# Second expert products and output in two column halves, with four more early load tiles

## The chip, the cores and the metric

The kernel runs on one core of one Trainium2 chip. The metric is device time in microseconds (us) of one execution; before the change the median of three runs is 603.16 us (601.11 to 605.01). One further execution was profiled, and every row below is from it. Time zero of the rows is the start of its span.

## What is computed

Three parts follow each other: a chunked attention over 4 x 8 heads of 768 positions, a dense layer with a rational function in its middle (512 to 2048 to 512), and a soft mixture of 8 experts. The last part matters here:

```python
slot_input = d.T @ x                      # 32 slots, 4 of each expert
for e in range(8):
    h = np.maximum(slot_input[e] @ w1[e], 0.0)   # 512 -> 1024
    slot_out[e] = h @ w2[e]                      # 1024 -> 512
c = softmax over the 32 slots of x @ phi
return c @ slot_out                              # 3072 x 512
```

All is float32. The experts' weights are 16 MB of `w1` and 16 MB of `w2`, the output is 6.3 MB.

## The kernel before, in words

Tokens are worked in 6 blocks (NBLK) of 512. For each block PE forms the hidden layer in 8 steps, ACT, DVE and POOL evaluate the rational function, and a running softmax over tokens collects the slot sums in `u_acc`. The dense layer's output weights are narrowed to float32 early in block 0, step by step, and each step's 512 KB is parked in DRAM (`wo_dr`) by a DMA on POOL's queue; they are wanted again at the end.

From the first step of the last block on, everything that the end needs is loaded: 8 tiles of `wo_dr`, 32 of `w1`, 32 of `w2`, each 128 x 1024 floats (512 KB). They stand in one list (`wants`, the order in which PE uses them), and `fill` (L513 on) takes the next of the list for each buffer that the main loop gives back. The buffers are those of the ordinary pools (q, a4, k, v, xt, win, T, S, g), so a load waits until the last user of its buffer is done, in the order of the fills; SP issues all of them, with at most eight of its DMAs under way.

After the last block comes the end stage, and all of the change but the early loads lies here:

- L639 to L654: `u_acc` is turned, multiplied with the `wo` tiles and spread to the experts.
- L666: first products of the experts, `h1 = slot_input @ w1`, four experts beside each other in four groups of 32 columns of the PE array, in two rounds (`eq`) of four experts. L676/L678 take the positive part, L683 turns it, L685/L687 copy it out as `hts`.
- L693 and L701: second products with `w2`, 512 columns wide, four experts side by side; the last four `w2` tiles (L701) are worked in pieces of 256 columns as each of them lands.
- L705/L706 copy the result out in two column halves (W = 256), L709 adds the four groups through the constant matrix `stack`, L710/L711 copy that to `so4`.
- L724: for each block and pair of 128-token rows the output is `c_all` (32 slots) times `so4`; L729 (ACT) and L731 (DVE) scale it by `csum` on the way from PSUM to SBUF; L732 sends 128 x 1024 floats, 12 DMAs of 512 KB, in runs of 4 KB.

In the end stage before the change the tile scheduler orders the engines. PSUM is 8 banks of 512 floats a partition: pool `ps_h` two tiles of two banks, `ps_l` one bank, `ps_m` three.

In SBUF, 16 KB of each partition are set aside by default for descriptors of the DMAs that POOL issues (`wo_dr`).

Of the kernel before, what the change touches and what calls it, by code (L numbers as in the profile page):

```python
# [12 lines left out]
AF = mybir.ActivationFunctionType  # L13
ALU = mybir.AluOpType
# [30 lines left out]
def tile_chunk_attention__rational__soft_moe(  # L45
# [28 lines left out]
    NBLK = NT // BLK  # L74
    TT = BLK // P
# [15 lines left out]
    p_win = Pool(ctx.enter_context(tc.tile_pool(name="p_win", bufs=2 * NSTEP)))  # L91
    p_xt = Pool(ctx.enter_context(tc.tile_pool(name="p_xt", bufs=4)))
# [7 lines left out]
    p_s2 = Pool(ctx.enter_context(tc.tile_pool(name="p_s2", bufs=1)))  # L100
    p_dr = Pool(ctx.enter_context(tc.tile_pool(name="p_dr", bufs=1, space=bass.MemoryType.DRAM)))
    p_sm = Pool(ctx.enter_context(tc.tile_pool(name="p_sm", bufs=1)))
    ps_h = Pool(ctx.enter_context(tc.tile_pool(name="ps_h", bufs=2, space=PSUM)))
    ps_l = Pool(ctx.enter_context(tc.tile_pool(name="ps_l", bufs=1, space=PSUM)))
    ps_m = Pool(ctx.enter_context(tc.tile_pool(name="ps_m", bufs=3, space=PSUM)))

    def bank(shape):
        return ps_m("m", shape)
# [33 lines left out]
    xt = {}  # L142
# [165 lines left out]
    win = {}  # L308
# [66 lines left out]
    def soft1(b):  # L375
        lgs = p_s2("s2", [P, BLK])
        ACT.activation(lgs, st["lg"], AF.Copy)
        lt = bank([P, BLK])
        PE.matmul(lt, lhsT=stack, rhs=lgs, start=True, stop=True)
        ct = bank([P, TT, NSLOT])  # L380
        for tt in range(TT):
            PE.matmul(ct[:, tt, :], lhsT=lgs[:, tt * P:tt * P + P], rhs=stack[:, 0:NSLOT], start=True, stop=True)
        old, neg_m = (run[:, n:n + 1] for n in ((2, 0) if b % 2 else (0, 2)))
        bm, db = p_sm("bm", [P, 1]), p_sm("db", [P, 1])
        DVE.tensor_reduce(bm, lt, AX.X, ALU.max)
        if b == 0:
            DVE.tensor_scalar(neg_m, bm, -1.0, None, ALU.mult)
        else:
            DVE.tensor_scalar(neg_m, bm, -1.0, old, ALU.mult, ALU.min)
            ACT.activation(alpha, old, AF.Exp, bias=neg_m, scale=-1.0)  # L390
        pl = p_s2("s2", [P, BLK])
        ACT.activation(pl, lt, AF.Exp, bias=neg_m, accum_out=db)
        if b == 0:
            DVE.tensor_copy(den, db)
        else:
            DVE.scalar_tensor_tensor(den, den, alpha, db, ALU.mult, ALU.add)
        cm = p_sm("cm", [P, TT])
        ce = p_sm("ce", [P, TT, NSLOT])
        DVE.tensor_reduce(cm, ct, AX.X, ALU.max)
        DVE.tensor_tensor(ce, ct, cm.unsqueeze(2).to_broadcast([P, TT, NSLOT]), ALU.subtract)  # L400
        ACT.activation(ce, ce, AF.Exp)
        DVE.tensor_reduce(csum[:, b * TT:b * TT + TT], ce, AX.X, ALU.add)
        st["pl"], st["ce"] = pl, ce

    def soft2(b):
        pl = st.pop("pl")
        pb = bank([P, TT, NSLOT])
        for tt in range(TT):
            PE.transpose(pb[:, tt, :], pl[0:NSLOT, tt * P:tt * P + P], ident[0:NSLOT, 0:NSLOT])
        st["ptok"] = p_sm("ptok", [P, TT, NSLOT])  # L410
        ACT.activation(st["ptok"], pb, AF.Copy)  # L411

    def soft3(b):
# [196 lines left out]
    for kk in range(total + 4):  # L610
        b, i = divmod(kk, NSTEP)
        if kk == last:
            fill(p_q, "q", 1, 1)
            fill(p_a4, "a4", 2, 1)
            fill(p_k, "k", 1, 2)
            fill(p_v, "v", 1, 2)
            fill(p_xt, "xt", 2, 2)
        if i == 0 and b < NBLK - 1:
            state["att"] = attention_block(b + 1)
        for what in KN["ord0" if b == 0 else "ord" if b < NBLK - 1 else "ordz" if kk == total - 1 else "ordl"]:  # L620
            run_step(kk, what)
# [38 lines left out]
    for eq in range(2):  # L660
# [29 lines left out]
    for eq in range(2):  # L690
        for n in range(8 - 2 * eq):
            for j in range(4):
                PE.matmul(so[32 * j:32 * j + 32, :], lhsT=hts[eq][:, n, 32 * j:32 * j + 32],  # L693
                          rhs=got[("2", 4 * eq + j, n // 2)][:, n % 2, :],
                          start=(eq == 0 and n == 0), stop=False)
    W = DM // 2
    for j in range(4):
        for n in range(2):
            for w in range(2):
                g = (j + 2 * n + w) % 4  # L700
                PE.matmul(so[32 * g:32 * g + 32, W * w:W * w + W], lhsT=hts[1][:, 6 + n, 32 * j:32 * j + 32],  # L701
                          rhs=got[("2", 4 + j, 3)][:, n, W * w:W * w + W],
                          start=False, stop=(j == 3))
    sos, so4 = u_acc.rearrange("p (w d) -> p w d", w=2), p_s2("s2", [P, 2, W])
    ACT.activation(sos[:, 0], so[:, 0:W], AF.Copy)  # L705
    DVE.tensor_copy(sos[:, 1], so[:, W:])  # L706
    pb = [bank([P, W]) for _ in range(2)]
    for w in range(2):
        PE.matmul(pb[w], lhsT=stack, rhs=sos[:, w], start=True, stop=True)  # L709
    ACT.activation(so4[:, 0], pb[0], AF.Copy)  # L710
    DVE.tensor_copy(so4[:, 1], pb[1])  # L711
    rows = out.rearrange("(b r t) d -> b r t d", r=P, t=TT)
    for b in range(NBLK):
        for half in range(2):
            ob = p_win("win", [P, 2, DM])
            if half:
                pb = [bank([P, DM]) for _ in range(2)]
            else:
                both = ps_h("h", [P, 2, DM])
                pb = [both[:, m, :] for m in range(2)]  # L720
            for m in range(2):
                g = 32 * (2 * half + m)
                for w in range(2):
                    PE.matmul(pb[m][:, W * w:W * w + W], lhsT=c_all[g:g + 32, b, :], rhs=so4[g:g + 32, w, :],  # L724
                              start=True, stop=True)
            for m in range(2):
                n = TT * b + 2 * half + m
                if (m if b == 0 else half):
                    ACT.activation(ob[:, m, :], pb[m], AF.Copy, scale=csum[:, n:n + 1])  # L729
                else:  # L730
                    DVE.tensor_scalar(ob[:, m, :], pb[m], csum[:, n:n + 1], None, ALU.mult)  # L731
            SP.dma_start(out=rows[b, :, 2 * half:2 * half + 2, :], in_=ob)  # L732


_INS = ['qw', 'kw', 'vw', 'moe_w_in', 'moe_w_out', 'moe_a', 'moe_b', 'moe2_phi', 'moe2_w1', 'moe2_w2']
# [58 lines left out]
```

## Time and profile before

| | us |
|---|---|
| median of three runs | 603.16 |
| the profiled execution's own time | 600.04 |
| its span, from first to last instruction | 598.1 |
| PE busy | 546.8 (91% of the span) |
| DVE busy | 455.6 (76%) |
| ACT busy | 417.3 (70%) |

The profiled execution is 3.12 us under the median; 1.94 us of it lie outside the span. Rows of the timeline give a start, a duration, engine, line, operation, tiles and how many instructions were merged; in brackets the idle time before and what ended it. One float32 product of the source is two PE instructions, so 4 products are x8. Rows of windows give the stretch, its length, the busy time of each engine with its instructions, the clock granted to PE (1.00 is 2.4 GHz, 0.50 is 1.2 GHz), the share of the 16 DMA engines that is busy, and GB/s.

### The profile page before, as it was taken

The numbers are of one execution on the slowest core, as the hardware profiler recorded it, in microseconds if no ns is written. First come the engines' busy times: TensorE is split into PE (matmuls) and PEld (weight loads), VectorE is DVE, ScalarE is ACT, GpSimd is POOL, SyncE is SP. The second block draws the span as 40 slices with busy tenths as digits, with TensorE's granted clock in tenths as the row PEclk, the third lists the DMA queues.
The fourth block names the chain that finished last, engine by engine and source line by source line (L and its number), as shares of the span: only waits on it lengthen the run. The fifth ranks groups of instructions, "written<-read, shape, count | busy, mean of one in ns | idle before, by whom it ended". The sixth has DMA issues, their size and how long they took to land.

```text
span 598.1 us, 13663 instructions
## 1 busy us (share of the span) xinstructions
PE 546.8 (91%) x5944; PEld 390.4 (65%) x5944; DVE 455.6 (76%) x561; ACT 417.3 (70%) x542; POOL 124.6 (21%) x65
## 2 busy tenths in 40 slices
PE   6799699889999999999999999999999998779982
PEld 5677576667767777677776777766777576326241
DVE  4778999976987989978899798896987968711032
ACT  1589989976876868768687777777787869420032
POOL 0001221211322223122231313222133225200000
PEclk9699799888999999999999999999999999889996
DMA  8888674410221112212122022220374334799949
GB/s 351 354 327 322 256 291 185 147 66 1 107 73 66 61 53 106 73 42 80 58 107 73 15 93 72 107 71 3 106 276 156 132 118 158 290 358 411 408 184 360
DMA packets 21371, 97.41 MB, mean 163 GB/s; under 512 B 2624, under 2 KB 2752, under 8 KB 16320
## 3 DMA queue, kind: packets, MB, share of 16 engines
q1 hardware_dynamic: 20160, 92.35, 41.4%
q0 software_dynamic: 1152, 4.19, 1.7%
q8 instruction: 46, 0.75, 0.5%
q14 instruction: 13, 0.11, 0.1%
HBM read 86.05 MB, written 10.49 MB: 161 GB/s over the span
## 4 chain that ended last, share of the span: by engine, by line
PE 59%; DVE 14%; ACT 11%; DMA 8%; issue 4%; POOL 2%; SPq 0%; ACTq 0%; DVEq 0%; POOLq 0%
PE h L342 30%; PE m L368 4%; PE m L419 4%; PE lg L361 3%; ACT S L566 3%; ACT S L567 3%; PE m L224 3%; PE m L445 2%; DMA g<-in_moe_w_in_dram 2%; DVE T L580 2%; DVE T L579 2%; DMA g<-in_moe_w_out_dram 2%; PE h L666 2%; ACT g L369 2%; DVE S L568 2%
## 5 line engine op out<-in xcount | busy, mean ns | idle before, releaser
L342 PE MATMUL h<-xt,win 128*128 128x512 f32 x1152 | 293.4, 403 | 7.5 <-ACT win L325 5.3
L342 PEld LDWEIGHTS h<-xt,win 128*128 128x128 f32 x1152 | 212.1, 191 | 54.8 <-ACT win L325 6.7
L543 POOL TENSOR_TENSOR S<-S,S 128x1024 f32<-128x1024 f32 (+1 forms) x49 | 118.3, 2416 | 306.9 <-DVE S L568 288.8
L566 ACT ACTIVATE S<-h,ctab 128x1024 f32<-128x1024 f32 (+1 forms) x49 | 53.9, 1100 | 58.3 <-PE h L342 56.3
L568 DVE SCALAR_TENSOR_TENSOR S<-S,S 128x1024 f32<-128x1024 f32 (+1 forms) x49 | 58.8, 1200 | 41.0 <-ACT S L567 40.9
L579 DVE TENSOR_TENSOR T<-T,h 128x1024 f32<-128x1024 f32 (+1 forms) x49 | 58.4, 1191 | 6.6 <-ACT T L569 6.6
L596 DVE SCALAR_TENSOR_TENSOR T<-T,ctab,S 128x1024 f32<-128x1024 f32 (+1 forms) x49 | 63.3, 1294 | 0.0
L368 PEld LDWEIGHTS m<-ident,T 128*128 128x128 f32 x384 | 44.3, 144 | 27.9 <-issue 13.6
L597 DVE SCALAR_TENSOR_TENSOR T<-S,T 128x1024 f32<-128x1024 f32 (+1 forms) x49 | 59.8, 1219 | 3.2 <-POOL S L543 0.5
L580 DVE SCALAR_TENSOR_TENSOR T<-T,ctab,h 128x1024 f32<-128x1024 f32 (+1 forms) x49 | 61.2, 1250 | 0.7
L569 ACT ACTIVATE T<-h,ctab 128x1024 f32<-128x1024 f32 (+1 forms) x49 | 59.1, 1206 | 0.0
L586 ACT ACTIVATE S<-S,ctab 128x1024 f32<-128x1024 f32 (+1 forms) x49 | 55.9, 1140 | 0.8
L585 ACT ACTIVATE S<-S 128x1024 f32<-128x1024 f32 (+1 forms) x49 | 51.6, 1053 | 6.7 <-DVE S L568 4.9
L368 PE MATMUL m<-ident,T 128*128 128x128 f32 x384 | 54.1, 282 | 2.1 <-DVE a L185 1.4
L369 ACT ACTIVATE g<-m 128x512 f32<-128x512 f32 x96 | 53.4, 601 | 3.1 <-PE m L368 3.0
L567 ACT ACTIVATE S<-h,ctab 128x1024 f32<-128x1024 f32 (+1 forms) x49 | 54.1, 1104 | 0.6 <-DVE T L596 0.6
L361 PE MATMUL lg<-T,wp 128*32 128x512 f32 x192 | 38.9, 614 | 5.4 <-DVE T L597 5.3
L186 ACT ACTIVATE a<-a 128x512 f32<-128x512 f32 x22 | 13.8, 634 | 19.5 <-DVE a L185 19.5
L419 PE MATMUL m<-g,ptok 128*32 128x512 f32 x192 | 23.5, 634 | 0.4 <-ACT ptok L411 0.4
L333 POOL DMA_DIRECT2D wo<-win x8 | 4.7, 588 | 86.7 <-DVE win L303 67.3
L248 DVE TENSOR_TENSOR xt<-m,xt 128x512 fp32r<-128x512 f32 x24 | 16.3, 687 | 8.1 <-ACT xt L247 8.0
L247 ACT ACTIVATE xt<-m 128x512 fp32r<-128x512 f32 x24 | 14.3, 607 | 9.7 <-PE m L243 9.7
(163 smaller groups left out, 626.6 us busy)
## 6 DMA issues: line engine op xcount, KB each, us to landing
win<-in_moe_w_dram SPq DMA_DIRECT2D x32, 512.0 KB, 6.0
k<-in_kw_dram SPq DMA_DIRECT2D x11, 1024.0 KB, 7.2
v<-in_vw_dram SPq DMA_DIRECT2D x11, 1024.0 KB, 4.9
g<-in_moe_w_in_dram SPq DMA_DIRECT2D x8, 1024.0 KB, 5.7
g<-in_moe_w_out_dram SPq DMA_DIRECT2D x8, 1024.0 KB, 8.4
out_dram<-win SPq DMA_DIRECT2D x12, 512.0 KB, 5.0
q<-in_qw_dram SPq DMA_DIRECT2D x11, 512.0 KB, 4.1
T<-in_moe_w_dram SPq DMA_DIRECT2D x10, 512.0 KB, 9.7
```

Source lines behind the costliest of these rows:

```text
L342: PE.matmul(tile_[:, f2, :], lhsT=ww[:, c, f2 * P:f2 * P + P], rhs=xx[:, c, :], start=(n == 0), stop=(n == 3 * NC - 1))
L368: PE.transpose(pb[:, m, f2 * P:f2 * P + P], t_[:, f2, tt * P:tt * P + P], ident)
L369: ACT.activation(gts[b, qd][:, 2 * part:2 * part + 2, 2 * P * o:2 * P * o + 2 * P], pb, AF.Copy)
L543: POOL.tensor_tensor(out[:, o], q[:, o], w[:, o], ALU.mult)
L566: ACT.activation(s[:, o], hh[:, o], AF.Abs, scale=b0)
L567: ACT.activation(y[:, o], hh[:, o], AF.Square, scale=rb1)
L568: DVE.scalar_tensor_tensor(s[:, o], y[:, o], QC, s[:, o], ALU.add, ALU.add)
L569: ACT.activation(t[:, o], hh[:, o], AF.Identity, bias=a2, scale=a3)
L579: DVE.tensor_tensor(t[:, o], t[:, o], hh[:, o], ALU.mult)
L580: behind[kk] = DVE.scalar_tensor_tensor(t[:, o], t[:, o], a1, hh[:, o], ALU.add, ALU.mult).ins
L596: DVE.scalar_tensor_tensor(t[:, o], t[:, o], a0, w[:, o], ALU.add, ALU.mult)
L597: DVE.scalar_tensor_tensor(t[:, o], e[:, o], 2.0, t[:, o], ALU.subtract, ALU.mult, reverse0=True)
```

## The change

The end stage works the second products, their sum and the output in two column halves, `w` = 0 and 1, each 256 wide. All 16 groups of products of half 0 come first (`items(0)`), then four groups of half 1, the sum of half 0, and then six times two groups of half 1 and one output pass of half 0. After that comes half 1: copy, sum and six output passes. An output pass (`output(w, pair, u)`) is two blocks by two 128-row groups in one `ps_h` tile of two banks; ACT scales the part in one bank, DVE that in the other, and two DMAs of 256 KB are sent, in runs of 1 KB. The order of PE, ACT and DVE in this part is written out by hand (`manual_schedule`).

A pool `p_x` of four tiles is added. It is first in the list of fills, and its buffers have no earlier user. Its room comes from 15 KB less descriptor scratch (1024 bytes) and from two small tiles: `ce` now lives in its place in `c_all`, `ptok` in the tile of `pl`.

```diff
@@
+    p_x = Pool(ctx.enter_context(tc.tile_pool(name="p_x", bufs=4)))
@@ soft1, soft2
-        ce = p_sm("ce", [P, TT, NSLOT])
+        ce = c_all[:, b, :].rearrange("p (t s) -> p t s", t=TT)
-        st["ptok"] = p_sm("ptok", [P, TT, NSLOT])
+        st["ptok"] = pl[:, 0:TT * NSLOT].rearrange("p (t s) -> p t s", t=TT)
@@
         if kk == last:
+            fill(p_x, "x", 4, 1)
             fill(p_q, "q", 1, 1)
@@
-    so = ps_l("lg", [P, DM])
...
+    so = [ps_l("lg", [P, W]), bank([P, W])]
+    so4 = p_s2("s2", [P, 2, W])
+    def items(w):
+        cols = slice(W * w, W * w + W)
+        for eq in range(2):
+            for n in range(8 - 2 * eq):
+                for j in range(4):
+                    PE.matmul(so[w][32 * j:32 * j + 32, :], lhsT=hts[eq][:, n, 32 * j:32 * j + 32],
+                              rhs=got[("2", 4 * eq + j, n // 2)][:, n % 2, cols], ...)
+                yield
+        for j in range(4):
+            for n in range(2):
...
+            if j % 2:
+                yield
+    def copy_up(w):
+        if w:
+            DVE.tensor_copy(sos[:, w], so[w])
+        else:
+            ACT.activation(sos[:, w], so[w], AF.Copy)
+    def sum_up(w):
+        pb = bank([P, W])
+        PE.matmul(pb, lhsT=stack, rhs=sos[:, w], start=True, stop=True)
...
+    def output(w, pair, u):
+        pb = ps_h("h", [P, 2, 2, W])
+        if u == 0:
+            obs[w] = p_xt("xt", [P, 2, 2, 2, W])
+        ob = obs[w][:, u]
+        for m in range(2):
+            for v in range(2):
+                g = 32 * (2 * u + v)
+                PE.matmul(pb[:, v, m, :], lhsT=c_all[g:g + 32, 2 * pair + m, :], rhs=so4[g:g + 32, w, :], ...)
+        for m in range(2):
+            b = 2 * pair + m
+            for v in range(2):
+                n = TT * b + 2 * u + v
+                if v:
+                    DVE.tensor_scalar(ob[:, m, v, :], pb[:, v, m, :], csum[:, n:n + 1], None, ALU.mult)
+                else:
+                    ACT.activation(ob[:, m, v, :], pb[:, v, m, :], AF.Copy, scale=csum[:, n:n + 1])
+            SP.dma_start(out=rows[b, :, 2 * u:2 * u + 2, W * w:W * w + W], in_=ob[:, m])
+    end.enter_context(tc.manual_schedule(engines={e.engine for e in (PE, ACT, DVE)}))
+    for _ in items(0):
+        pass
+    copy_up(0)
+    rest = items(1)
+    for _ in range(4):
+        next(rest)
+    sum_up(0)
+    for n in range(NBLK):
+        for _ in range(2):
+            next(rest, None)
+        output(0, n // 2, n % 2)
+    for _ in rest:
+        pass
+    copy_up(1)
+    sum_up(1)
+    for n in range(NBLK):
+        output(1, n // 2, n % 2)
@@
-    nc = _bacc.Bacc("TRN2", target_bir_lowering=False, num_devices=1)
+    nc = _bacc.Bacc("TRN2", target_bir_lowering=False, num_devices=1, dynamic_dma_scratch_size=1024)
```

How the instructions stand. On SP, in block 0, the loads of raw weights (`g`) and of attention (`v`) before the change:

```order
L317 DMA g_858<-in_moe_w_out_dram 128x2048
L312 DMA g_870<-in_moe_w_in_dram 128x2048
L135 DMA v_970<-in_vw_dram 128x2048
L317 DMA g_1021<-in_moe_w_out_dram 128x2048
L312 DMA g_1033<-in_moe_w_in_dram 128x2048
```

And after it, with the four loads of the new pool (`x`) from the parked weights (`wo`):

```order
L318 DMA g_861<-in_moe_w_out_dram 128x2048
L527 DMA x_5119<-wo_137 128x1024
L527 DMA x_5121<-wo_137 128x1024
L527 DMA x_5123<-wo_137 128x1024
L313 DMA g_873<-in_moe_w_in_dram 128x2048
L136 DMA v_973<-in_vw_dram 128x2048
L318 DMA g_1024<-in_moe_w_out_dram 128x2048
L527 DMA x_5125<-wo_137 128x1024
L313 DMA g_1036<-in_moe_w_in_dram 128x2048
```

Three of the new loads stand after the same `g` load, the fourth one `g` load later; each can go only when its `wo` tile has been written.

On PE, the end before the change (`lg` is the second products' bank, `m` a `ps_m` bank, `h` a `ps_h` tile, `call` is `c_all`, `s` is `so4`):

```order
L701 MATMUL lg_5958<-T_5936,k_5945 32x256 x4
L701 MATMUL lg_5958<-T_5938,k_5945 32x256 x4
L701 MATMUL lg_5958<-T_5940,k_5945 32x256 x4
L709 MATMUL m_6034<-u_107,stack_104 128x256
L709 MATMUL m_6035<-u_107,stack_104 128x256
L724 MATMUL h_6041<-s_15_6031,call_110 128x256
L724 MATMUL m_6050<-s_15_6031,call_110 128x256
```

After the change, from the last products of half 0 (`lg`) the four groups of half 1 (`m_5951`) follow; the rows from the end of the fourth to the first output pass are:

```order
L700 MATMUL m_5951<-S_5754,q_5877 32x256
L700 MATMUL m_5951<-g_5756,q_5877 32x256 x2
L700 MATMUL m_5951<-g_5759,q_5877 32x256
L723 MATMUL m_6036<-u_110,stack_107 128x256
L700 MATMUL m_5951<-g_5759,q_5877 32x256
L700 MATMUL m_5951<-g_5762,q_5877 32x256 x2
L700 MATMUL m_5951<-g_5765,q_5877 32x256
L700 MATMUL m_5951<-g_5759,q_5877 32x256
L700 MATMUL m_5951<-g_5762,q_5877 32x256 x2
L700 MATMUL m_5951<-g_5765,q_5877 32x256
L740 MATMUL h_6047<-s_15_5952,call_113 128x256 x4
```

The products of half 1 now stand behind the last tile's, before and between the output passes (L740), where L724 stood alone.

On DVE, the end before the change (L706/L711 the copies of the second half, L731 the scaling of the output):

```order
L706 COPY u_107<-lg_5958 128x256
L711 COPY s_15_6031<-m_6035 128x256
L731 TENSOR_SCALAR win_6040<-h_6041,csum_108 128x512
L731 TENSOR_SCALAR win_6049<-m_6050,csum_108 128x512
L731 TENSOR_SCALAR win_6059<-h_6060,csum_108 128x512 x2
```

And after it, in the middle of the output (L747 the scaling, L717 and L725 the copies of half 1):

```order
L747 TENSOR_SCALAR xt_6126<-h_6125,csum_111 128x256 x2
L747 TENSOR_SCALAR xt_6126<-h_6145,csum_111 128x256 x2
L717 COPY u_110<-m_5951 128x256
L725 COPY s_15_5952<-m_6157 128x256
L747 TENSOR_SCALAR xt_6161<-h_6160,csum_111 128x256 x2
```

The copy of half 1 stands behind the last scaling of half 0, and every `h` tile is now read by DVE and ACT both (L749, likewise x2 per pass).

## Rows read from the trace of the kernel before

**Rows 1.** Windows over the end: columns as under "Time and profile before".
```profile
520.00:540.00 20.00, 15.45 (x103) 6.58 (x107) 3.70 (x19) 4.57 (x11) 0.95 (x1) 0.91 0.80 310
540.00:574.60 34.60, 32.03 (x280) 13.58 (x274) 2.89 (x6) 2.39 (x4) 0.00 (x0) 1.00 0.97 387
574.60:580.90 6.30, 5.25 (x53) 3.58 (x54) 3.16 (x6) 2.29 (x5) 0.00 (x0) 1.00 0.00 0
580.90:596.50 15.60, 5.31 (x62) 4.66 (x55) 5.80 (x9) 6.03 (x10) 0.00 (x0) 0.75 1.02 403
596.50:598.10 1.60, 0.00 (x0) 0.00 (x0) 0.00 (x0) 0.00 (x0) 0.00 (x0) 0.50 0.00 0
```

**Rows 2.** The chain that ended last, around the last loads.
```profile
564.44 10.12 DMA T<-in_moe_w_dram
...
574.60 0.68 PE lg L701 x8
```

**Rows 3.** Timeline of SP's queue: last loads and output.
```profile
559.33 5.43 SPq L526 DMA_DIRECT2D T<-in_moe_w_dram  x5
580.09 13.03 SPq L732 DMA_DIRECT2D out_dram<-win  x12
```

**Rows 4.** Timeline of PE in the end stage.
```profile
557.62 0.63 PE L693 MATMUL lg<-g,q 128*32 128x512 f32 x3
...
558.62 0.66 PE L683 MATMUL m<-ident,a 128*128 128x128 f32 x4
559.21 2.78 PE L693 MATMUL lg<-g,q 128*32 128x512 f32 x24
...
572.11 0.64 PE L701 MATMUL lg<-T,k 128*32 128x256 f32 x8 [0.23 <-DMA T<-in_moe_w_dram]
573.37 0.64 PE L701 MATMUL lg<-T,k 128*32 128x256 f32 x8 [0.62 <-DMA T<-in_moe_w_dram]
...
575.75 1.16 PE L709 MATMUL m<-u,stack 128*128 128x256 f32 x4 [0.50 <-ACT u L705]
...
577.74 0.38 PE L724 MATMUL h<-s,call 32*128 32x256 f32 x2
...
577.96 0.38 PE L724 MATMUL h<-s,call 32*128 32x256 f32 x2
```

**Rows 5.** Timeline of ACT, then of DVE, in the end stage.
```profile
575.31 0.38 ACT L705 ACTIVATE u<-lg 128x256 f32<-128x256 f32 x1 [15.40 <-PE lg L701]
576.48 0.38 ACT L710 ACTIVATE s<-m 128x256 f32<-128x256 f32 x1 [0.79 <-PE m L709]
579.38 0.69 ACT L729 ACTIVATE win<-h,csum 128x512 f32<-128x512 f32 x1 [2.51 <-DVE win L731]
...
575.73 0.42 DVE L706 COPY u<-lg 128x256 f32<-128x256 f32 x1 [17.30 <-ACT u L705]
578.59 0.75 DVE L731 TENSOR_SCALAR win<-h,csum 128x512 f32<-128x512 f32 x1 [1.23 <-PE m L724]
```

**Rows 6.** Timeline of SP's queue in block 0, a load behind the new ones.
```profile
79.87 0.33 SPq L312 DMA_DIRECT2D g<-in_moe_w_in_dram  x1
```

**Rows 7.** Timeline of ACT in block 0, where that load's tile is worked.
```profile
97.58 1.15 ACT L299 ACTIVATE g<-g 128x1024 uint32<-128x1024 uint32 x1
```

**Rows 8.** Timeline of SP's queue at the start, two small loads.
```profile
6.84 0.33 SPq L267 DMA_DIRECT2D ctab<-in_moe_b_dram  x1
8.12 0.33 SPq L268 DMA_DIRECT2D u<-in_moe_phi_dram  x1
```

**Rows 9.** DMA issues: KB each and us to landing, of the same two loads.
```profile
u<-in_moe_phi_dram SPq DMA_DIRECT2D x1, 64.0 KB, 14.3
ctab<-in_moe_b_dram SPq DMA_DIRECT2D x1, 1.0 KB, 15.3
```

**Rows 10.** Windows around a fall of PE's clock.
```profile
523.90:527.40 3.50, 1.82 (x20) 0.78 (x24) 1.50 (x9) 1.44 (x5) 0.00 (x0) 0.98 1.01 407
527.40:530.70 3.30, 3.30 (x20) 0.83 (x16) 0.00 (x0) 0.00 (x0) 0.00 (x0) 0.50 1.02 417
```

More of the change, by code (lines that the diff above doesn't have):

```diff
@@ L688, in tile_chunk_attention__rational__soft_moe @@
         hts.append(hT)
-    so = ps_l("lg", [P, DM])
[L690 to L695, printed above, removed]
-    W = DM // 2
[L697 to L711, printed above, removed]
-    rows = out.rearrange("(b r t) d -> b r t d", r=P, t=TT)
[L713 to L729, printed above, removed]
-                else:
-                    DVE.tensor_scalar(ob[:, m, :], pb[m], csum[:, n:n + 1], None, ALU.mult)
-            SP.dma_start(out=rows[b, :, 2 * half:2 * half + 2, :], in_=ob)
@@ new lines, in tile_chunk_attention__rational__soft_moe @@
+    W = DM // 2
+    so = [ps_l("lg", [P, W]), bank([P, W])]
[6 more added lines that the diff above has]
+                    PE.matmul(so[w][32 * j:32 * j + 32, :], lhsT=hts[eq][:, n, 32 * j:32 * j + 32],
+                              rhs=got[("2", 4 * eq + j, n // 2)][:, n % 2, cols],
+                              start=(eq == 0 and n == 0), stop=False)
+                yield
+        for j in range(4):
+            for n in range(2):
+                g = (j + 2 * n) % 4
+                PE.matmul(so[w][32 * g:32 * g + 32, :], lhsT=hts[1][:, 6 + n, 32 * j:32 * j + 32],
+                          rhs=got[("2", 4 + j, 3)][:, n, cols],
+                          start=False, stop=(j >= 2))
+            if j % 2:
+                yield
@@ new lines, in tile_chunk_attention__rational__soft_moe @@
+    sos = u_acc.rearrange("p (w d) -> p w d", w=2)
+    def copy_up(w):
[6 more added lines that the diff above has]
+        PE.matmul(pb, lhsT=stack, rhs=sos[:, w], start=True, stop=True)
+        if w:
+            DVE.tensor_copy(so4[:, w], pb)
+        else:
+            ACT.activation(so4[:, w], pb, AF.Copy)
+    rows = out.rearrange("(b r t) d -> b r t d", r=P, t=TT)
@@ new lines, in tile_chunk_attention__rational__soft_moe @@
+    obs = {}
+    def output(w, pair, u):
[6 more added lines that the diff above has]
+                g = 32 * (2 * u + v)
+                PE.matmul(pb[:, v, m, :], lhsT=c_all[g:g + 32, 2 * pair + m, :], rhs=so4[g:g + 32, w, :],
+                          start=True, stop=True)
+        for m in range(2):
[4 more added lines that the diff above has]
+                    DVE.tensor_scalar(ob[:, m, v, :], pb[:, v, m, :], csum[:, n:n + 1], None, ALU.mult)
+                else:
+                    ACT.activation(ob[:, m, v, :], pb[:, v, m, :], AF.Copy, scale=csum[:, n:n + 1])
+            SP.dma_start(out=rows[b, :, 2 * u:2 * u + 2, W * w:W * w + W], in_=ob[:, m])
@@ new lines, in tile_chunk_attention__rational__soft_moe @@
+    end = ExitStack()
+    end.enter_context(tc.manual_schedule(engines={e.engine for e in (PE, ACT, DVE)}))
[16 more added lines that the diff above has]
+        output(1, n // 2, n % 2)
+    end.close()
```

## The prediction

> **What bounds the kernel now.** I read the windows over the end first, then the chain, then the timelines of PE, ACT, DVE and SP. The change to the main loop is small, so only the end and the early loads are priced. The windows [rows 1] show three stretches. Up to 540 us the DMA engines are not full (share 0.80): loads wait for buffers. From 540 to the last load they are full (0.97, with an emptying tail), while PE still has work nearly all the time. Then from 574.60 to 580.90 nothing moves at all; from 580.90 to 596.50 the output runs at 403 GB/s with a share of 1.02, and 1.60 us later the span ends. The chain [rows 2] agrees: a load issued at 564.44 takes 10.12 us, since eight stand in the queue, and PE's last products start at 574.60. So the end is a full stretch of loading, 6.3 us without transfers, and a full stretch of storing. The change attacks the first (fewer late bytes) and the second (the first half sent earlier).
>
> **Early loads.** Four tiles of 512 KB leave the late list; of five last loads into T [rows 3] one is left. While the queue is full their time is 4 x 0.524 MB = 2.10 MB at 403 to 414 GB/s (the latter is eight tiles in the 10.12 us of rows 2), 5.1 us. I take all of it: the win buffers are given back a little later in PE's order (the list is shifted by four), but eight loads stand queued, which is 10 us of cover. The last products of half 0 start at 574.60 - 5.1 = 569.5. In block 0 the new loads cost 2.1 MB and a wait on SP for the parked tile, the fourth possibly in front of the load issued at 79.87 [rows 6]. Its tile is worked at 97.58 at the earliest [rows 7], so a delay of a microsecond or two is covered by over ten; without that cover it would cost what it is late. I take 0. The smaller scratch serves eight DMAs that POOL issues far apart; the in-place softmax tiles only lengthen lives of buffers whose next user comes a block later. Both 0.
>
> **The tail, step by step.** Prices first. Four products of 512 columns beside each other are eight instructions; 24 took 2.78 us with the tail of the last [rows 4], so a group is 0.86, and of 256 columns 0.43. Where PE changes the form (128x32 to 128x128), eight instructions of L693 last from 557.62 to 558.62 and the four turns from 558.62 to 559.21; against 0.86 and 0.44 that is 0.14 per change. The output's products run two by two, a pair of instructions every 0.22 (577.74, 577.96) [rows 4], and there are eight of them per pass: 0.86. Copying 256 columns takes ACT 0.38 and DVE 0.42, the hand-over from one to the other 0.04 (575.31 + 0.38 to 575.73) [rows 5]. From the start of a `stack` product to the copy it is 0.73 (575.75 in rows 4 to 576.48 in rows 5).
>
> Half 0: last products 569.5 to 569.95, four groups of half 1 (1.72) and a change, so the sum starts at 571.8, and `so4` is there at 571.8 + 0.73 + 0.38 + 0.04 = 572.95. PE meanwhile does sum and two groups with two changes, 571.8 + 0.57 + 1.00 = 573.4, so the copy is hidden. Output pass 0.86 and 0.2 to drain: 574.45.
>
> Here a new wait enters. Where ACT and DVE read the same `h` tile, the second waits for the first: L729 stood 2.51 us and started at 579.38, when DVE's L731 had just ended (578.59 + 0.75 = 579.34) [rows 5]. After the change every pass has four such parts, ACT, DVE, ACT, DVE: 0.38 + 0.42 + 0.38 + 0.42 + 3 x 0.04 = 1.72 for a pass; the next pass's first ACT part overlaps the last DVE part, so passes follow at 0.42 + 0.04 + 0.38 + 0.04 + 0.42 = 1.30. The first DMA goes after two parts, at 574.45 + 0.90 = 575.35, against 580.09 [rows 3].
>
> But half 0 is not sent at full rate. Each pass stands on PE behind two groups of half 1: 0.86 + 0.14 + 0.86 + 0.14 = 2.0 us per 512 KB, where the DMA engines need 1.30. Five more passes end their products at 584.45, the scaling at 586.2. Behind that on DVE stands the copy of half 1 (586.6), and behind the copy PE's sum: 586.65 + 0.73 + 0.42 = 587.8. Then a pass (0.86 + 0.2): 588.9, five more at 1.30 (595.4), and the last one's 1.72: 597.1. The last 256 KB need 0.8 from issue to first data (580.09 to 580.90, rows 3 and 1) and 0.65 at 403 GB/s: 598.55, and 1.60 to the end of the span: 600.15. That is 2.05 more than 598.1: 7 us of half 1's products now lie behind the last load, and they and the hand-overs use up the 5.1 us of loading and the overlap. The profiled execution's own time goes from 600.04 to 602.1; its 3.12 us to the median added, 605.2.
>
> **Unknown: rows of 1 KB.** No output of the kernel before is sent in runs under 4 KB. Lower end: no loss (403 GB/s). Upper end by the nearest small rows: the 64 KB load with runs of 512 bytes was issued at 8.12 and took 14.3, the one ahead 6.84 and 15.3 [rows 8, 9], so it landed 0.28 later; that is 230 GB/s if those 0.28 are all its own, roundings included. Half 1 (3.15 MB) would then take 13.7 instead of 7.8 us, 5.9 more. I take 0, since both times are rounded to 0.1 and both loads sat in a full queue, and keep 5.9 for the range. The Trainium skill, page "DMA: Bandwidth & Descriptors", section "Why small descriptors are slow (HBM only)", speaks against the change: some three cycles of the engine's inner bus go to each packet beside one for 32 bytes, which by that rule is 35 cycles for 1 KB against 32; no run here shows it yet. By it the stores would be about 7% slower and the sum about 0.5 us higher, an estimate from that page.
>
> **Rivals.**
> A. The overlap works as meant. If the changes of form and the hand-overs cost nothing and PE kept ahead, the stores would run without a gap from 575.35: 0.8 + 15.6 + 1.6 gives a span of 593.3, 4.8 less, 598.4 us. For it: the stores alone need just 15.6 us [rows 1]. Against it: PE's 2.0 per pass holds even with free hand-overs.
> B. PE's clock falls while it waits for the last tiles, since half 0's products are done as fast as tiles land. In the trace the clock fell to 0.50 after a stretch with PE busy 1.82 of 3.50 us and stayed there 3.3 us under full work [rows 10]. After the change each tile brings 0.43 of work per 1.28 us. Against it: the same trickle at the end before (572.11, 573.37, rows 4) went by at 1.00 [rows 1], though for under 3 us. Price: 3.3 us at half speed lose 1.65, 606.9.
> C. The 1 KB rows set the end: slower. Place: the stores of half 1. It decides from 403 GB/s downward, and at 230 GB/s it costs 5.9: 611.1. For it: that pair of landings; against it: their roundings.
> D. The loads end no earlier, because the late stretch waits for buffers after all: 2.05 + 5.1, 610.3. Against it: the full queue [rows 1, 2].
>
> **How the numbers follow.** Forecast 0.50, A 0.20, B 0.15, C 0.10, D 0.05. A measurement of this kernel can tell about 1%, 6 us, from no change. Forecast and B lie within it, but for a twentieth that ends above 609.2; of A a good third would lie beyond 1% faster with the scatter of runs. C ends above in seven of ten cases, D always. So faster 0.07, same 0.76, slower 0.17. The range goes from 599.5, which leaves out the full gain of A, to 609.5, which takes in part of C; the forecast's own is 602.5 to 607.5.
>
> **What would show it.** Right: the last products of half 0 at about 569.5; the first output DMA at about 575.4; output passes of half 0 every 2.0 us and a DMA share near 0.65 there; a gap of some 3 us without stores about 588; passes of half 1 every 1.3 us; ACT and DVE waiting for each other in all of it. Wrong: stores without a gap (A), a clock under 1.00 between 565 and 575 (B), a share of 1 with clearly under 400 GB/s in half 1 (C), the last load at 574 (D).

## The result, and the profile after

The changed kernel takes 610.66 us (median of four runs, 606.31 to 612.85), the kernel before 603.33 on the same chip; the ratio is 1.0139, 95% interval 1.0092 to 1.0185. So it is slower by 0.9 to 1.9%, where 605.2 (599.5 to 609.5) and no measurable change were forecast. The profiled execution took 611.64 us with a span of 609.8.

The windows over the end, cut where [rows 1] are cut (last loads, no transfers, output, the two halves of the output apart):

```profile
520.00:540.00 20.00, 16.12 (x95) 6.04 (x93) 3.93 (x13) 4.38 (x11) 0.95 (x1) 0.83 0.72 275
540.00:573.58 33.58, 28.52 (x276) 15.16 (x276) 3.51 (x12) 2.92 (x5) 0.00 (x0) 1.00 0.93 365
573.58:580.30 6.72, 6.72 (x84) 3.71 (x86) 0.57 (x2) 1.72 (x4) 0.00 (x0) 1.00 0.00 0
580.30:593.00 12.70, 9.55 (x106) 4.96 (x106) 5.99 (x13) 4.75 (x10) 0.00 (x0) 1.00 0.72 249
593.00:609.00 16.00, 8.75 (x48) 5.74 (x44) 5.53 (x12) 5.37 (x12) 0.00 (x0) 0.50 0.56 197
```

Half 0 goes out at 249 GB/s, as PE feeds it. From 593 to 596 nothing is stored (share 0.00). The stretch of half 1 comes to 197 GB/s, with the DMA engines busy 0.56 of the time and PE's clock at 0.50 from 593 on. SP's queue in the same stretch:

```profile
533.74 3.73 SPq L527 DMA_DIRECT2D g<-in_moe_w_dram  x8
544.12 0.80 SPq L527 DMA_DIRECT2D v<-in_moe_w_dram  x2
545.96 16.51 SPq L527 DMA_DIRECT2D win<-in_moe_w_dram  x16
563.42 0.33 SPq L527 DMA_DIRECT2D T<-in_moe_w_dram  x1
579.70 27.37 SPq L750 DMA_DIRECT2D out_dram<-xt  x24
```

The same loads before the change, which the forecast had not shown:

```profile
531.36 3.73 SPq L526 DMA_DIRECT2D g<-in_moe_w_dram  x8
537.38 0.80 SPq L526 DMA_DIRECT2D v<-in_moe_w_dram  x2
541.88 16.51 SPq L526 DMA_DIRECT2D win<-in_moe_w_dram  x16
```

The main loop ends a few us earlier or later from execution to execution (531.36 and 533.74 here, 527.00 to 537.26 in the runs below). To compare stages I therefore count from the first of these `g` loads. The `v` loads come 6.0 us behind it before the change and 10.4 behind it after. PE at the end, last tile, first and last pass of half 0, sum and passes of half 1:

```profile
573.58 0.41 PE L707 MATMUL lg<-T,k 128*32 128x256 f32 x2 [0.63 <-DMA T<-in_moe_w_dram]
...
577.50 1.13 PE L740 MATMUL h<-s,call 32*128 32x256 f32 x8
579.56 1.13 PE L740 MATMUL h<-s,call 32*128 32x256 f32 x8
...
587.81 1.13 PE L740 MATMUL h<-s,call 32*128 32x256 f32 x8
591.49 0.67 PE L723 MATMUL m<-u,stack 128*128 128x256 f32 x2 [2.54 <-DVE u L717]
592.77 2.00 PE L740 MATMUL h<-s,call 32*128 32x256 f32 x16 [0.61 <-DVE s L725]
596.81 3.49 PE L740 MATMUL h<-s,call 32*128 32x256 f32 x16 [2.05 <-DVE xt L747]
601.05 3.49 PE L740 MATMUL h<-s,call 32*128 32x256 f32 x16 [0.75 <-DVE xt L747]
```

Passes of half 0 follow at 2.06 us. In half 1 two passes come together (x16, both `h` tiles) and pairs follow at 4.24 us. ACT, then DVE, at the start of half 0 and in the second pair of half 1, and DVE's last part:

```profile
578.67 0.47 ACT L749 ACTIVATE xt<-h,csum 128x256 f32<-128x256 f32 x1 [1.69 <-PE h L740]
579.70 0.47 ACT L749 ACTIVATE xt<-h,csum 128x256 f32<-128x256 f32 x1 [0.55 <-DVE xt L747]
...
598.98 0.47 ACT L749 ACTIVATE xt<-h,csum 128x256 f32<-128x256 f32 x1 [1.32 <-PE h L740]
...
579.18 0.48 DVE L747 TENSOR_SCALAR xt<-h,csum 128x256 f32<-128x256 f32 x1 [18.40 <-ACT xt L749]
...
600.51 0.88 DVE L747 TENSOR_SCALAR xt<-h,csum 128x256 f32<-128x256 f32 x2 [0.54 <-ACT xt L749]
...
606.18 0.48 DVE L747 TENSOR_SCALAR xt<-h,csum 128x256 f32<-128x256 f32 x1 [0.54 <-ACT xt L749]
```

They take strict turns: DVE starts at 579.18 when ACT's part has ended at 579.14, ACT at 579.70 when DVE's has ended at 579.66.

In half 1 each `h` tile goes through a loop. PE begins to fill one at 596.81, ACT starts on it 2.17 us later (598.98), the four parts take their turns (DVE's last one is the first of the two at 600.51), and at 601.05 PE fills the tile again: 2.17 + 2.07 = 4.24 us. With two tiles this makes two passes per 4.24 us.

The stages, in us from the first `g` load (forecast: its times less 531.36). The last two columns are the runs e13 and e15 below:

| | before | forecast | after | e13 | e15 |
|---|---|---|---|---|---|
| products with the last tile start | 43.24 | 38.14 | 39.84 | 39.87 | 38.42 |
| first output DMA | 48.73 | 43.99 | 45.96 | 45.54 | 44.09 |
| first pass of half 1 on PE | – | 56.44 | 59.03 | 57.88 | 57.03 |
| last scaling ends | – | 65.74 | 72.92 | 65.77 | 65.82 |
| end of the span | 66.74 | 68.79 | 76.06 | 71.14 | 70.28 |

After the change the span ends 7.27 us behind the forecast: 1.70 at the last tile, 0.27 up to the first DMA, 0.62 up to half 1, 4.59 in half 1, 0.09 behind it.

### The profile page after: what moved, and what is told of

The parts are those of the page before. It is cut to its first block, busy times and chain, and to the rows that moved or that the text cites. A ratio compares the mean times of both kernels' runs of the same rounds, so it can differ in the third digit from the quotient of the medians.

```text
span 609.8 us, 13945 instructions
## 1 busy us (share of the span) xinstructions
PE 557.4 (91%) x6056; PEld 396.6 (65%) x6056; DVE 459.0 (75%) x573; ACT 421.8 (69%) x554; POOL 124.7 (20%) x65
## 4 chain that ended last, share of the span: by engine, by line
PE 60%; DVE 14%; ACT 12%; DMA 6%; issue 5%; POOL 2%; SPq 0%; ACTq 0%; DVEq 0%; POOLq 0%
PE h L343 30%; PE m L369 4%; PE m L420 4%; PE lg L362 4%; DMA win<-in_moe_w_dram 3%; ACT S L567 3%; ACT S L568 3%; PE m L225 2%; ACT g L370 2%; DVE T L580 2%; PE h L740 2%; DVE S L569 2%; DVE T L581 2%; POOL S L544 2%; PE m L446 2%
## 5 line engine op out<-in xcount | busy, mean ns | idle before, releaser
L747 DVE TENSOR_SCALAR xt<-h,csum 128x256 f32<-128x256 f32 x24 | 11.3, 483 | 32.9 <-ACT xt L749 32.9
L420 PE MATMUL m<-g,s 128*32 128x512 f32 x192 | 23.2, 626 | 0.4 <-ACT s L412 0.4
L749 ACT ACTIVATE xt<-h,csum 128x256 f32<-128x256 f32 x24 | 11.1, 474 | 18.1 <-PE h L740 11.4
```

## Experiments

All ratios are to the kernel before, run beside them; intervals are 95%.

| run | edit | median us | ratio |
|---|---|---|---|
| e1 | before + early tiles alone | 597.90 | 0.9977 (0.994 to 1.0014) |
| e2 | halves alone | 614.66 | 1.0255 (1.0206 to 1.0305) |
| e6 | before + runs of 1 KB | 604.76 | 1.0062 (1.0026 to 1.0097) |
| e3 | after + gap filled | 608.37 | 1.0147 (1.0106 to 1.0188) |
| e4 | after, copy and sum of half 1 earlier | 611.20 | 1.0181 (1.0127 to 1.0235) |
| e5 | after, one engine a pass | 612.14 | 1.0195 (1.0142 to 1.0249) |
| e8 | after, gap filled, three products ahead of each pass | 607.66 | 1.0129 (1.0074 to 1.0184) |
| e11 | after, gap filled, one product ahead of each pass | 607.34 | 1.0111 (1.0068 to 1.0154) |
| e7 | before + last tiles early | 598.00 | 0.9942 (0.9906 to 0.9978) |
| e9 | e7 + first tile in two banks | 597.61 | 0.9955 (0.9919 to 0.9992) |
| e10 | after, last tiles early | 610.78 | 1.0165 (1.0095 to 1.0234) |
| e12 | e10 + e11 | 606.76 | 1.0089 (1.0045 to 1.0133) |
| e13 | after, own tile for each engine | 605.03 | 1.0064 (1.0024 to 1.0103) |
| e14 | e13 + gap filled | 605.55 | 1.0070 (1.0024 to 1.0116) |
| e15 | e14 + last tiles early | 603.38 | 1.0029 (0.9992 to 1.0067) |

### The parts by themselves: early tiles, halves, 1 KB runs

e1 adds `p_x`, its fill, the smaller scratch and the moved small tiles to the kernel before; e2 is the changed kernel without them; e6 splits each DMA of the kernel before:

```diff
-            SP.dma_start(out=rows[b, :, 2 * half:2 * half + 2, :], in_=ob)
+            for w in range(2):
+                SP.dma_start(out=rows[b, :, 2 * half:2 * half + 2, W * w:W * w + W], in_=ob[:, :, W * w:W * w + W])
```

> The kernel before with the four early tiles alone (new pool, smaller scratch, the two small tiles moved); the tail is that of before. Theory tail: the loss lies in the new tail and the early tiles help, though less than the 5.1 us forecast, because the v buffers now hold w1 tiles and come free 6 us later; last load 2 to 3.5 us earlier than before, time 2 to 3.5 us under before, last products at 571 to 572.5. Rival early: the early tiles themselves cost, in block 0 or by the shifted list; no faster than before, or slower by 1 to 3 us.

> The changed kernel without the four early tiles (no new pool, scratch and small tiles as before); the tail is the new one. Theory tail: the last load is where it was before (574.6), and from there to the end it takes the 36 us of the changed kernel instead of 23.5, so 9 to 13 us over before, 2 to 3.5 over the changed kernel. Rival early: without the early tiles the loss shrinks, 2 to 6 us over before, and faster than the changed kernel.

> The kernel before with each of the 12 output DMAs sent as two, one per column half, so 24 of 256 KB in runs of 1 KB instead of 4 KB; nothing else. From the changed kernel's rows (342 GB/s at a share of 0.99 against 403 at 1.02) the stores of 6.3 MB last 18.3 us instead of 15.6: 2.5 to 3 us over before. Rival none: runs of 1 KB cost nothing when the queue is full, within 0.7 us of before. Rival dear: they set the changed kernel's end, and cost 6 us or more.

e1: the last load is issued 2.5 us earlier than before (30.60 us behind the first `g` load for 33.08), but the first DMA goes at 47.34, only 1.39 earlier, not 5, and the ratio (0.9977) can't be told from 1. Windows at the end of its loads:

```profile
566.00:568.00 2.00, 2.00 (x25) 0.65 (x20) 0.00 (x0) 0.00 (x0) 0.00 (x0) 1.00 0.35 133
568.00:570.00 2.00, 2.00 (x35) 1.04 (x30) 0.00 (x0) 0.00 (x0) 0.00 (x0) 1.00 0.01 4
```

The loads are in at 567, but PE is busy all of 568 to 570: in the order of before PE has full work behind the loads, and what they can give is what PE waits for them. That is 0.23 + 0.62 [rows 4] + 0.59 = 1.44 us; the third wait stands in the row behind those two, in the trace of before:

```profile
574.60 0.64 PE L701 MATMUL lg<-T,k 128*32 128x256 f32 x8 [0.59 <-DMA T<-in_moe_w_dram]
```

e2 costs 2.6%, some 14 us, without early tiles (9 to 13 were expected). Its clock also fell while PE waited for the last tiles, as rival B had it, which in the changed kernel it did not:

```profile
581.00:584.00 3.00, 3.00 (x30) 1.49 (x25) 0.00 (x0) 0.39 (x1) 0.00 (x0) 0.50 0.00 0
```

e6: the stores run at a full share with 339 to 343 GB/s in place of 403 [rows 1]. The span ends 3.1 us later against the first `g` load (69.87 for 66.74), but 0.4 of it lie ahead of the first output DMA (49.10 for 48.73). From that DMA to the end of the span it is 20.77 us for 18.01, so the short runs cost 2.8:

```profile
590.00:593.00 3.00, 0.00 (x0) 0.00 (x0) 0.00 (x0) 0.00 (x0) 0.00 (x0) 0.50 1.02 341
593.00:596.00 3.00, 0.00 (x0) 0.00 (x0) 0.00 (x0) 0.00 (x0) 0.00 (x0) 0.50 1.01 343
```

### Half 1: the gap, the clock or the turns

e3 puts `busy(9)` (nine needless products) ahead of `copy_up(1)`; e4 spreads half 1's products in threes over four passes, and copies half 1 ahead of the last two passes of half 0 and sums it between them; e5 gives a pass to one engine; e8 adds `busy(9)` in the gap and `busy(3)` ahead of each pass of half 1, e11 the same with `busy(1)`:

```diff
# e5
-                if v:
+                if u:
                     DVE.tensor_scalar(ob[:, m, v, :], pb[:, v, m, :], ...)
# e8, e11
+    busy(9)
     copy_up(1)
     sum_up(1)
     for n in range(NBLK):
+        busy(3)
         output(1, n // 2, n % 2)
```

> The changed kernel with nine products of the identity (2 us of PE work into the free lg bank, read by nobody) in PE's gap between the two halves. Theory clock: PE's clock falls in that gap and makes each output pass of half 1 last 2.1 us on PE instead of 1.0; with the gap filled the clock stays at 1.00, passes of half 1 follow each other at 1.5 us instead of 2.1, and the time falls by 3 to 5 us against the changed kernel. Rival store: half 1 is paced by its stores in runs of 1 KB; passes stay at 2.1 us or more and the time at that of the changed kernel, within 1 us.

> The changed kernel, but the products of half 1 run in threes between the first four passes of half 0, and copy and sum of half 1 stand between its last two passes, so that no engine stands still between the halves. In the changed kernel PE does nothing from 588.9 to 591.5 and most of 592, its clock is 0.50 from 593 on, and the twelve parts of half 1 take 13.9 us. Theory that the gap lets the clock fall: without it the clock stays at 1.00 in half 1, passes of half 1 follow at 1.3 to 1.55 us, and the time falls by 5 to 6 us (ratio to the changed kernel 0.990). Rival, that the pace of half 1 itself (PE waiting for the h tiles that ACT and DVE read in turn) lets it fall: the clock is 0.50 in half 1 all the same, pairs of passes take 4.24 us, and only 1 to 2 us of the gap are won.

> The changed kernel, but each output pass is scaled by one engine alone (ACT the first of a pair, DVE the second), so that no part waits for the other engine's part. Theory that the hand-overs between ACT and DVE on one h tile set the pace: a pair of passes takes four parts of one engine, 1.9 us, and PE's share before them, 2.5 to 3.0 us in place of 4.24, the clock holds, and 3 to 4 us are won. Rival, that at half clock PE's own 3.49 us per pair set the pace: pairs take 3.5 to 4.2 us and under 1.5 us are won.

> The changed kernel with needless products on PE: nine in the gap between the halves and three ahead of each output pass of half 1. Theory that the clock sets the pace of half 1: it stays at 1.00, passes of half 1 follow at 1.5 to 1.6 us, the rate at which 512 KB in runs of 1 KB can be stored (342 GB/s), the twelve parts of half 1 take about 9.5 us in place of 13.9, and the time falls by about 4 us. Rival, that the hand-overs alone set the pace: pairs of passes still take over 4 us at a clock of 1.00 and nothing is won.

> The changed kernel with needless products on PE, nine in the gap between the halves and only one (0.28 us) ahead of each pass of half 1, so that they can't set the pace themselves as three did (1.93 us per pass). Theory that the clock and then the hand-overs set it: at a clock of 1.00 four parts in turn, 0.47 and 0.48 with two hand-overs between, give 1.54 us per pass, the twelve last DMAs go within 10.0 us of the first product of half 1 in place of 13.9, and the ratio to before is about 1.007. Rival, that so few products don't hold the clock: pairs of passes at 4.24 us again, ratio as with the gap alone filled, 1.0147.

e3: with the gap filled the first two passes run at full clock, and then it falls all the same:

```profile
589.31 1.16 PE L740 MATMUL h<-s,call 32*128 32x256 f32 x16 [0.61 <-DVE s L725]
592.56 3.49 PE L740 MATMUL h<-s,call 32*128 32x256 f32 x16 [2.08 <-DVE xt L747]
596.80 3.50 PE L740 MATMUL h<-s,call 32*128 32x256 f32 x16 [0.75 <-DVE xt L747]
```

The first pass to the last scaling takes 13.1 us (13.9 after the change). In e4 PE still waits 1.78 us for the copy of half 1 (2.54 after the change); its clock is 0.50 from 586 on, with pairs at 4.20 us. In e5 pairs take 3.80 us at 0.50, since PE now waits until one engine has done all four parts of a tile; nothing is won. None of the three ratios can be told from the changed kernel's 1.0139. So the gap alone is not the cause: e3 filled it, and the clock fell behind it. e5 could not tell the turns from the clock.

e8 holds the clock at 1.00 to the end of the products; its passes follow at 1.93 us, which is PE's own 1.06 and 0.87 of needless products, and half 1 takes 12.8 us in place of the 9.5 that were expected. e11 leaves PE room and shows the pace at a clock of 1.00. PE at the start of two pairs, then ACT's first part of the earlier one:

```profile
590.97 1.13 PE L740 MATMUL h<-s,call 32*128 32x256 f32 x8 [0.21 <-DVE xt L747]
594.27 1.13 PE L740 MATMUL h<-s,call 32*128 32x256 f32 x8 [0.27 <-DVE xt L747]
...
592.20 0.47 ACT L749 ACTIVATE xt<-h,csum 128x256 f32<-128x256 f32 x1 [0.31 <-PE h L740]
```

From 590.97 to 594.27 a pair takes 3.30 us, 1.65 per pass (1.54 expected, 1.30 forecast, 2.12 after the change). It is the same loop of one tile: 1.23 us from PE's start to ACT's, 2.07 of turns as after the change. From the first product to the last DMA issue it is 11.3 us, where 10.0 were expected. The ratios of e8 and e11 can't be told from the changed kernel's either.

### Early tiles without a shift

e7 (end stage of before) and e10 (end stage of after) load the last four tiles of `w2` into `p_x` in the third block, behind a `k` load on SP's queue, and work them ahead of the others of their round, so that all other tiles keep their buffers. e9 adds to e7 that the first output tile stands in two banks of `ps_m`, and that ACT alone scales the second. e12 is e10 with e11's needless products.

```diff
-    wants += [("2", 4 * eq + j, n) for eq in range(NE // 4) for n in range(4) for j in range(4)]
+    wants += [("2", 4 * eq + j, n) for eq in range(NE // 4) for n in range(4 - eq) for j in range(4)]
+    wants_x = [("2", 7 - j, 3) for j in range(4)]
...
+        if kk == 2 * NSTEP + 2:
+            with tc.issue_after(loaded["qk"]):
+                fill(p_x, "x", 4, 1, wants_x)
...
-        for n in range(8 - 2 * eq):
+        for n in [range(8), (6, 7, 0, 1, 2, 3)][eq]:
# e9
-            if half:
+            if half != (b == 0):
                 pb = [bank([P, DM]) for _ in range(2)]
...
-                if (m if b == 0 else half):
+                if (m if b == half == 0 else half):
```

> The end stage of before, with the four tiles of the new pool, but they hold the last four tiles of w2 (loaded in block 3, worked ahead of the others of their round) and not the first four parked tiles, so that every other tile keeps the buffer that it had before the change. Theory that the early tiles lost most of their worth because the list was shifted into buffers that are given back later (v, xt, win): now the four loads are gone from the end of the full stretch, the last products end 5.1 us earlier than before against the first late load, and the ratio to before is about 0.9915. Rival, that the late stretch waits for buffers in any case: 1 to 1.5 us, ratio 0.9977 as with the first four parked tiles.

> The kernel with the end stage of before and the last four tiles loaded early, and one more edit: the first output tile is formed in two separate PSUM banks, so that ACT and DVE scale its two parts at the same time. Before, ACT stood 2.51 us and started only when DVE's part of the same h tile was done. Theory that two engines reading one PSUM tile wait for each other: the first output DMA goes 0.5 to 0.7 us earlier and the span is shorter by that, ratio to before about 0.993. Rival, that the order of the products or something else held ACT: the first DMA stays 47.5 us behind the first late load, ratio 0.994.

> The changed kernel, but the four early tiles are the last four of w2 (loaded in block 3, worked ahead of the others of their round), so that no other tile changes its buffer. In the changed kernel PE waits for tiles six times near the end, 3.46 us in all, in the order of before three times, 1.44 us. Theory that early tiles are worth what PE waits for the last tiles: here 3 to 3.5 us are won (1.4 in the order of before), the last products of half 0 start 36.3 to 37 us behind the first late load in place of 39.8, and the ratio to before falls from 1.014 to about 1.008. Rival, that what is won is given back in the clock, which falls before the end of the loads or in the output: under 1.5 us.

> Both edits together: the last four tiles early in the changed order, and the needless products (nine in the gap, one ahead of each pass of half 1). Theory that the miss is the sum of the late loads and of half 1 at half clock: 7 us less than the changed kernel, ratio to before about 1.002, that is the time that was forecast. Rival, that one takes the place of the other: no better than the better of the two alone, 1.007.

e7: the theory falls. The `v` loads are back at 6.0 us and the last load is issued 4.3 us earlier than before (28.75 for 33.08), yet the first DMA goes only 1.2 us earlier (47.51). PE had no more than those 1.44 us to win. In e10, where PE has half the products before the first output, the last tile's products start 38.25 us behind the first `g` load, against 43.21 in e2, where PE waits 4.4 us for tiles: 4.96 for the four tiles, 3.4 of them left (39.84) with the shift. Against the changed kernel that is 1.6 us, where 3 to 3.5 were expected, and PE still waits 2.8 us for tiles. The time shows no gain (1.0165): the 1.6 us are inside the interval.

e9: ACT and DVE start side by side and the first DMA goes 3.23 us behind the start of the sum (574.55 to 577.78), in e7 4.35; 0.5 to 0.7 were expected of this edit. On ACT, then DVE:

```profile
577.00 0.69 ACT L734 ACTIVATE win<-m,csum 128x512 f32<-128x512 f32 x1 [1.33 <-PE m L729]
...
576.96 0.75 DVE L736 TENSOR_SCALAR win<-m,csum 128x512 f32<-128x512 f32 x1 [0.79 <-PE m L729]
```

Its 1.1 us are too small for the ratio (0.9955 against 0.9942). e7 and e9 are both faster than the kernel before, by half a per cent, and e9's profile ends 62.8 us behind the first `g` load, the earliest of all.

e12 keeps the clock at 1.00 and the early loads. Its ratio (1.0089) is 0.5% under the changed kernel's, which is inside the intervals, and not the 1.2% expected: the turns remain, and the stores are at 347 GB/s with a share of 1.02 when they end.

### The turns alone

Open at that point was what leaves PE idle in half 1. e13 gives ACT's and DVE's parts a PSUM tile each; e14 also fills the gap; e15 adds e10's early tiles.

```diff
-        pb = ps_h("h", [P, 2, 2, W])
+        pb = ps_h("h", [P, 2, W]), bank([P, 2, W])
...
-                    ACT.activation(ob[:, m, v, :], pb[:, v, m, :], AF.Copy, scale=csum[:, n:n + 1])
+                    ACT.activation(ob[:, m, v, :], pb[v][:, m, :], AF.Copy, scale=csum[:, n:n + 1])
```

> The changed kernel, but each output pass has two PSUM tiles of one bank, one for ACT's parts and one for DVE's, in place of one h tile of two banks, so that the two engines scale at the same time. Theory that the turns on one tile make PE idle and the idle PE lets the clock fall: a pass of half 1 is then held only by its slowest engine, PE's 1.06 us at a clock of 1.00 (1.75 at 0.50) or two parts of 0.48, and the stores of 1.5 us per 512 KB set the pace; the clock holds; from the first product of half 1 to the last DMA issue 9.5 to 10 us in place of 14.0, ratio to before 1.006 to 1.008. Rival, that the gap between the halves alone lets the clock fall: the clock is 0.50 all through half 1, passes then follow at 1.75 us, 2 us are won, ratio about 1.010. Third, that the turns don't matter: 4.24 us per pair and a ratio of 1.014.

> The same with nine needless products in the gap between the halves. Theory that only gap and turns together let the clock fall: 1.00 all through half 1, passes at 1.5 us by the stores' rate, 9.5 to 10 us from the first product of half 1 to the last DMA issue, ratio to before 1.005 to 1.008. Rival, that PE falls idle behind the stores (at a share of two thirds) and the clock falls in any case: it is 0.50 before the end of half 1, but at 1.75 us per pass that costs under 1 us.

> The same as the last, with the last four tiles of w2 loaded early in place of the first four parked ones. Theory that the miss is the sum of shifted early loads, turns and clock: 1.5 us less than the run before, ratio to before 1.002 to 1.005, which is the time that was forecast. Rival, that the order in two halves still costs more than that for another reason: ratio over 1.008.

e13: the engines scale at the same time, four parts (two passes) in 1.6 us. ACT, then DVE:

```profile
591.87 1.56 ACT L749 ACTIVATE xt<-h,csum 128x256 f32<-128x256 f32 x4 [2.90 <-PE m L740]
593.97 1.57 ACT L749 ACTIVATE xt<-h,csum 128x256 f32<-128x256 f32 x4 [0.54 <-ACT xt L749]
...
591.91 1.66 DVE L747 TENSOR_SCALAR xt<-m,csum 128x256 f32<-128x256 f32 x4 [1.32 <-PE m L740]
594.03 1.66 DVE L747 TENSOR_SCALAR xt<-m,csum 128x256 f32<-128x256 f32 x4 [0.45 <-issue]
```

Pairs follow at 2.1 us, and the clock is 1.00 until about 595.6. Half 1 takes 7.9 us from its first product to its last scaling (13.9 after the change), without any needless product. From 594 on the stores run without a pause and set the end:

```profile
594.00:596.00 2.00, 1.76 (x16) 1.28 (x15) 1.66 (x4) 1.54 (x4) 0.00 (x0) 0.89 1.01 339
596.00:598.00 2.00, 1.67 (x10) 0.77 (x6) 1.13 (x3) 1.14 (x3) 0.00 (x0) 0.50 0.98 341
598.00:600.00 2.00, 0.00 (x0) 0.00 (x0) 0.62 (x2) 0.54 (x2) 0.00 (x0) 0.50 1.00 340
```

e14 adds nothing to the ratio: the gap costs nothing once the turns are gone. Its clock stays at 1.00 to the end of the products, but in the profiled execution it was down earlier, at 0.50 from 571 to 573 while PE worked the last tile, for which it had waited 1.43 us:

```profile
570.92 0.64 PE L707 MATMUL lg<-T,k 128*32 128x256 f32 x2 [1.43 <-DMA T<-in_moe_w_dram]
```

e15 comes to 1.0029, as expected (1.002 to 1.005): no longer told from the kernel before, and still not faster. In its half 1 the clock is 0.50 from 592 on, although the gap is filled and each engine has its tile:

```profile
592.00:594.00 2.00, 2.00 (x14) 1.23 (x14) 0.92 (x3) 0.92 (x3) 0.00 (x0) 0.50 1.02 342
```

Half 1 takes 8.8 us there (first product at 57.03, last scaling at 65.82), against 13.9 after the change, where the clock was down from the first pair on, in e15 from the second. So most of what e13 won is due to the turns themselves and not to the clock. The span of e15 ends 3.5 us behind that of before in the table above, though its first DMA goes 4.6 us earlier: PE still feeds half 0 at 2.06 us per pass, the stores pause between the halves, and in half 1 the 1 KB runs cost some 1.4 us (an estimate: 3.15 MB at 342 in place of 403 GB/s).

## Why the prediction was wrong

**Half 1's passes at 1.30 us: the step that failed most, 4.59 us.** The forecast had the turns of ACT and DVE on one `h` tile, but it took the pace from their parts alone and let PE's filling be hidden. There are only two `h` tiles, and PE can fill one again only when all four parts have left it. So two passes take the filling of a tile and its turns, one behind the other; by the forecast's own prices that is 0.86 + 0.2 + 1.72 + 0.04 = 2.82 us, 1.41 per pass. Two sizes were too small as well. A part was priced by the 256-column copies, 0.38 and 0.42, where a scaling that starts alone takes 0.47 and 0.48; with this the turns take 2.07, the filling 1.23, and a pair 3.30 at a clock of 1.00 (e11). The clock does the rest: the forecast had it at 1.00 in half 1, it is 0.50, the filling takes 2.17 in place of 1.23, and a pair takes 4.24, 2.12 per pass. Taking the turns away gave back 6.0 us of half 1 (e13), and 5.1 with the clock down from the second pair on (e15); holding the clock gave 2.7 (e11: from 13.9 to 11.2), filling the gap alone 0.8 (e3). That the turns make PE idle and the idle PE slow fits e3 and e13, but it is not all: in e15 the clock fell without turns, in e14 it held, and why is not shown.

**Rival B** had the right mechanism in the wrong place. Where I looked for it, waiting for the last tiles, the clock stayed at 1.00 in the changed kernel, and fell in e2 and e14. In e14 the way from the last tile to the first DMA took 7.1 us for 5.7 in e13, so the price of 1.65 was about right. I had not asked where else PE would be idle. In e3 PE waits 2.08 us for a tile that DVE holds, and the clock is 0.50 from there to the end of the products. The Trainium skill, page "TensorE: Matmul & The Clock Gate", section "A second HAM failure mode: psum-queue depth-cycling", tells of a bf16 kernel that cycles through PSUM banks, where PE's short pauses between groups of products make the clock swing between its two levels. The rows of e3 agree in kind, but show the clock staying down.

**Early loads, 5.1 us: 1.70 too many.** Without a shift the halves' order gets 4.96 (e10 against e2), so the price by the full queue was about right there. But I took the shift to concern the win buffers alone, with ten us of cover; it also moved `w1` tiles into the `v` buffers, which are loaded 4.4 us later, behind the products of `w1` (L668), and the queue ran part empty (0.93 over the loads in place of 0.97 [rows 1]). In the order of before, the same 5.1 us would have been wrong for another reason: PE waited for tiles 1.44 us in all. Block 0, put at nothing, cost nothing: from the `q` load at 47.50 to the one at 86.00 it is 38.50 us before the change, 38.44 after (50.66 to 89.10).

**Half 0, first DMA, sum of half 1: right.** Passes at 2.06 (2.0), 6.12 from the last tile to the first DMA (5.85), 13.07 from there to half 1 (12.45), and some 3 us without stores between the halves, as forecast. A share of 0.72, not 0.65, carries the same bytes: runs of 1 KB keep the engines longer (e6: 341 GB/s at a share of 1.02, before 403 at 1.02).

**The 1 KB runs (rival C)** cost 2.8 us by themselves (e6), 342 for 403 GB/s, 15% less; I took none, with 5.9 as the bound for half 1 alone. In the changed kernel they cost next to nothing (0.09 us behind the last scaling), since the stores waited for ACT and DVE. The Trainium skill, page "DMA: Bandwidth & Descriptors", section "Why small descriptors are slow (HBM only)", had given the forecast an estimate of 7%; what e6 measures is twice that.

**Rival A** does not hold even without turns: in e15 PE's products of half 1 between the passes still hold half 0 to 2.06 us per pass, as the forecast said against it. **Rival D** is refuted: the products with the last tile start 3.4 us earlier.

What stays open: the runs scatter by 1%, so that of the single edits only those of 4 us or more show in a ratio by themselves; what e1, e3, e4, e5, e8 to e12 and e14 say of their edits rests on one trace each. What sets off the fall of the clock in half 1 is open.

## What to carry to other kernels

Price an earlier load by what the consumer waits for it, not by the queue it leaves: of 1.44 us of PE's waits, e1 and e7 won 1.2 to 1.4, where the queue promised 5.1. Whoever moves the list of loads must follow each buffer to its last user. A pace between engines that share tiles is the loop of one tile, its filling and its draining one behind the other, divided by the number of tiles; the busiest engine alone gives too little. Two engines that drain PSUM want a tile each; taking turns on one tile costs their sum, and PE's clock, which was down in the same stretch, adds to the filling. Before splitting an output into column halves, measure the shorter runs by themselves: they can eat the overlap that the split was made for.

## What the runs showed that was not expected

ACT and DVE wait for each other on an `h` tile although their parts lie in different banks; with separate tiles they run side by side (e9: 576.96 and 577.00). The Trainium skill, page "PSUM — Partial Sum Buffer", section "PSUM bank collisions raise a hardware error", asks for a guard by bank and group of 32 partitions, or more simply by bank. The wait here was by tile, over both banks, and so more than that.

The same scaling of 128x256 is cheaper in a row than alone: four in 1.56 us on ACT and 1.66 on DVE (0.39 and 0.42 each), 0.47 and 0.48 where each starts behind the other engine. Two passes of a pair use different rows of the PE array (`g` 0 and 32, then 64 and 96). Where both tiles are free they run side by side, x16 in 1.16 us (e3, 589.31), as long as one alone (x8 in 1.13); where the second tile must be waited for, that is lost. Stores in runs of 1 KB keep the DMA engines fully busy (1.01) at 339 to 343 GB/s, those of 4 KB move 403.
